# A softmax convolution with a cosine FFN: steady exponentials by arithmetic on ScalarE and POOL, a different order of PE's products in every other period, output sums in place

## The chip, the cores and the metric

The kernel runs on one core of one Trainium2 chip. The metric is the device time of one execution in microseconds (us); less is better. Engines are named as in the profile: PE (TensorE, with PEld for its weight loads), DVE (VectorE), ACT (ScalarE), POOL (GpSimd) and SP (SyncE, which issues the DMAs).

## The reference

Two stages. The first mixes, for every token and head, the last 7 tokens with softmax weights; the second is an FFN whose activation is h·cos(h).

```python
# x (8, 4096, 192), weight_gen (8, 4096, 8 heads, 7 taps)
w = weight_gen - np.max(weight_gen, axis=-1, keepdims=True)
w = np.exp(w)
w = w / (np.sum(w, axis=-1, keepdims=True) + 1e-09)
x_pad = np.concatenate([np.zeros((B, pad, D)), x], axis=1)     # pad = 6
x_unf = x_pad[:, idx, :].reshape(B, S, K, H, group)            # the 7 last rows
out = np.einsum('bshk,bskhg->bshg', w, x_unf)                  # (B*S, 192) = x of the FFN
...
h = x @ w_in            # 192 x 2048
g = h * np.cos(h)
return g @ w_out        # 2048 x 192
```

## The kernel before

**Tiling.** The 32768 tokens are laid out as 128 partitions by 256 rows. A block is 4 rows (`R`), 512 tokens; there are 64 blocks (`NB`). The 2048 hidden features are 16 chunks of 128, taken two at a time: 8 pairs (`NPAIR`). The main loop runs over `i`, one *period* for each block and pair, 512 periods and a tail; `b, pair = divmod(i, 8)`. Matmuls are split into a leading part and a remainder (`x_hi`, `x_lo`; `ghi`, `glo`; `wa_hi`, `wa_lo` and so on).

**A period.** PE makes the hidden products of pair `i` in two groups, `ffn_in_first` (L339) and `ffn_in_second` (L356), into one of three PSUM tiles `h`, and eight periods later (`LAG`) the output products of pair `j = i - 8` (`ffn_out`, L430) into the PSUM tile `acc`. Between them lies the cosine: ACT `turn` (L366, h in whole turns as an integer), DVE fraction (L370), ACT sine (L374), DVE product (L377), ACT `ghi` (L384), DVE `glo` (L388). The last one frees the `h` tile, and PE's first product three periods later takes it again.

**Groups of four.** `k` is the place of `j` within four output periods, and equals `i` modulo 4. After k=1 ACT copies the transposed row out of `acc` into `xrow` and writes zeros over it (L446, L447 in `evacuate`); after k=3 it copies `acc` into `part` (L452) and POOL adds its two halves into `fin` (L461), which SP stores three periods later. The row of the next block but one is transposed by PE inside the output products (L318), then split by ACT (`x_hi`, L296) and POOL (`x_b`, L298, and `x_lo`, L301).

**PE's order in a period** is set in `products` (L597). With k=0 the period begins with the first hidden product, then all output products; with k=1, 2, 3 it begins with most of the output products, then the first hidden product, then the rest of the output products. The second hidden product is last in both.

**The first stage.** POOL forms the convolution of a block in 7 products (L255) and 6 sums (L270), two operations a period, under `bg`. The weights of 16 rows (four blocks) come from one `softmax` (L185): a DMA of `taps`, the maximum on DVE (L198), the subtraction on POOL (L200), `Exp` on ACT (L203), the sums on POOL (`add_taps`), a reciprocal on DVE (L214), and the final product on POOL (L220). It is a generator, moved on one step by the loop at the steps listed in `SOFTMAX`, once every 32 periods; `early=False` marks the 15 softmaxes of the loop. Around the `Exp` of step 6 the loop has special cases (`exps`, `early_sums`, held-back `splits`).

Every engine works through its instructions in the order in which the program issues them; a chain of dependencies at the end of the program fixes that order. SP stands between PE's product groups: `traded` (L281) lets PE's next group into a tile only after SP has seen the one before finished.

Of the kernel before, what the change touches and what calls it, by code (L numbers as in the profile page):

```python
# [11 lines left out]
F32 = mybir.dt.float32  # L12
F32R = mybir.dt.float32r
I32 = mybir.dt.int32
U16 = mybir.dt.uint16
BF16 = mybir.dt.bfloat16
AF = mybir.ActivationFunctionType
ALU = mybir.AluOpType
AX = mybir.AxisListType

P = 128
TWO_PI = 2.0 * math.pi
# [15 lines left out]


F64_SCALE = 2.0 ** -112  # L40


@with_exitstack
def tile_softmax_conv_then_cos_ffn(
# [8 lines left out]
    nc = tc.nc  # L53

    B, S, D = x.shape
    H, K = weight_gen.shape[2], weight_gen.shape[3]
# [5 lines left out]
    R = 4  # L62
    NB = RPP // R
# [3 lines left out]
    RW = 16  # L67
    SB = RW // R
    NPAIR = NFC // 2
# [10 lines left out]
    work = ctx.enter_context(tc.tile_pool(name="work", bufs=2))  # L80
# [6 lines left out]
    o_v = out.rearrange("(n q r) d -> q n (r d)", n=B, r=RPP)  # L87

    ident = const.tile([P, P], F32, name="ident")
    early = const.tile([P, 1], F32, name="early")  # L90
# [83 lines left out]
    taps, ready = {}, set()  # L174

    def add_taps(t, out):
        three_ = work.tile([P, RW * H, 3], F32, name="three", bufs=1)
        three = three_[:, 0:t.shape[1]]
        nc.gpsimd.tensor_tensor(out=three, in0=t[:, :, 0:3], in1=t[:, :, 3:6], op=ALU.add)
        old = three[:, :, 0]  # L180
        for more in (three[:, :, 1], three[:, :, 2], t[:, :, 6]):
            nc.gpsimd.tensor_tensor(out=out, in0=old, in1=more, op=ALU.add)
            old = out

    def softmax(r0, r1, eng, early=True, to=None):  # L185
        n = (r1 - r0) * H
        if r0 == 0:
            t = const.tile([P, n, K], F32, name="taps0")
        else:
            tile_ = work.tile([P, RW * H, K], F32, name="taps")  # L190
            t = tile_[:, 0:n, :]
        nc.sync.dma_start(out=t.rearrange("p a k -> p (a k)"), in_=g_v[:, :, r0 * H * K:r1 * H * K])
        for b in range(r0 // R, r1 // R):
            taps[b] = t.rearrange("p (r h) k -> p r h k", h=H)[:, b * R - r0:(b + 1) * R - r0]
        yield
        top_ = work.tile([P, RW * H], F32, name="top", bufs=1)
        top = top_[:, 0:n]
        nc.vector.tensor_reduce(out=top, in_=t, axis=AX.X, op=ALU.max)  # L198
        yield
        eng.tensor_tensor(  # L200
            out=t, in0=t, in1=top.unsqueeze(2).broadcast_to([P, n, K]), op=ALU.subtract)
        yield
        nc.scalar.activation(out=t, in_=t, func=AF.Exp)  # L203
        yield
        den_ = work.tile([P, RW * H], F32, name="den")
        den = den_[:, 0:n]
        if early:
            nc.vector.tensor_reduce(out=den, in_=t, axis=AX.X, op=ALU.add)
        else:
            add_taps(t, den)  # L210
        (nc.vector if early else nc.gpsimd).tensor_scalar(
            out=den, in0=den, scalar1=1e-9, scalar2=TWO_PI, op0=ALU.add, op1=ALU.mult)
        yield
        nc.vector.reciprocal(out=den, in_=den)  # L214
        yield
        m = 0 if to is None else to.shape[1]
        if m:
            eng.tensor_tensor(
                out=to, in0=t[:, 0:m], in1=den[:, 0:m].unsqueeze(2).broadcast_to([P, m, K]), op=ALU.mult)
        eng.tensor_tensor(  # L220
            out=t[:, m:], in0=t[:, m:], in1=den[:, m:].unsqueeze(2).broadcast_to([P, n - m, K]),
            op=ALU.mult)
        ready.update(range(r0 // R, r1 // R))
# [167 lines left out]
    accs, stores, splits = {}, {}, []  # L391
# [48 lines left out]
    def evacuate(j):  # L440
        b, tp, k = place(j)
        acc = accs[b, tp]
        row = row_of(j)
        if k == 1 and row:
            t = work.tile([P, 2, P], F32, name="xrow", bufs=2)
            nc.scalar.copy(out=t, in_=acc[:, :, 2 * D:])  # L446
            nc.scalar.copy(out=acc[:, :, 2 * D:], in_=zero.unsqueeze(2).broadcast_to([P, 2, P]))  # L447
        if k == 3:
            accs.pop((b, tp))
            part = work.tile([P, 2, CT], F32, name="part", bufs=2)  # L450
            width = CT if row else 2 * D
            nc.scalar.copy(out=part[:, :, 0:width], in_=acc[:, :, 0:width])  # L452
            t = part[:, :, 2 * D:]
        if k in (1, 3) and row:
            bt, r = row
            splits.append(split(bt, t, slice(r * P, (r + 1) * P), nc.gpsimd))
        if k < 3:
            return
        last = b == NB - 1
        fin = work.tile([P, 2, D], F32, name="fin")  # L460
        (nc.vector if last else nc.gpsimd).tensor_tensor(  # L461
            out=fin, in0=part[:, :, 0:D], in1=part[:, :, D:2 * D], op=ALU.add)

        def store():
            r0 = b * R + 2 * tp
            nc.sync.dma_start(out=o_v[:, :, r0 * D:(r0 + 2) * D],
                              in_=fin.rearrange("p r d -> p (r d)"))

        if last:
            store()  # L470
        else:
            stores[j + LATE] = store
        if tp == 1:
            for pair in range(NPAIR):
                g_parts.pop(b * NPAIR + pair)
# [59 lines left out]
    def go_on(steps, n):  # L535
        for _ in range(n):
# [4 lines left out]
                      t=own_taps.rearrange("p (r h) k -> p r h k", h=H))  # L541
# [28 lines left out]
    N = NB * NPAIR  # L570

    sm = sm2
    EXP = 6
    SOFTMAX = (0, 2, 3, EXP, 7, 12, 13)
    for i in range(N + LAG + 1):
        b, pair = divmod(i, NPAIR)
        j = i - LAG
        step = i % (SB * NPAIR) - (SB - 1) * NPAIR
        if step < 0 and i >= SB * NPAIR:
            step += SB * NPAIR  # L580
        if step == 0 and b + 4 < NB:
            r0 = (b + 4) * R
            sm = softmax(r0, min(r0 + RW, RPP), nc.gpsimd, early=False)
        busy = b + 4 < NB if step < NPAIR else b + 3 < NB
        exps = busy and step == EXP
        converts_now = converts.get(i, ())
        if converts_now:
            make_room()

        whole = None  # L590
        if pair == TR and b + 1 <= WHOLE:
            until_mixed(b + 1)
            whole = transpose_all(b + 1)
        if 0 <= j and (i - ROWS_AT) % (2 * R) == 0 and row_of(j):
            until_mixed(row_of(j)[0])

        def products():  # L597
            if b < NB and pair == 0:
                assert b in transposed
            if whole is not None and j >= 0:  # L600

                ffn_out(j)
                ffn_in_first(i, whole)
            elif i < N and j >= 0 and j % R != 0:

                ffn_out(j, rest=False)
                ffn_in_first(i)
                ffn_out(j, rest=True)
            else:
                if i < N:  # L610
                    ffn_in_first(i, whole)
                if j >= 0:
                    ffn_out(j)
            if i < N:
                ffn_in_second(i)
            if j in stores:
                stores.pop(j)()
            if j >= 0:
                evacuate(j)


        early_sums = busy and step == EXP + 1
        if 0 <= i - 1 < N:
            act_turns(i - 1)
        if early_sums:
            products()
        if 0 <= i - 2 < N:
            act_hi(i - 2)
        all_of(*converts.pop(i - 1, ()))
        if exps:  # L630
            next(sm)
        now, later = [], []
        if not (busy and EXP + 1 <= step <= EXP + 3):
            now = list(splits)
            splits.clear()
        if whole is not None:
            t = work.tile([P, 2, CT], F32, name="part", bufs=2)
            nc.scalar.copy(out=t, in_=whole)
            later.append(split(b + 1, t, slice(0, CT), nc.vector))
        if 0 <= i - 1 < N:  # L640
            dve_fraction(i - 1)
            act_cos(i - 1)
        for c in now:
            next(c)
        splits.extend(later)
        if 0 <= i - 2 < N:
            dve_lo(i - 2)
        if 0 <= i - 1 < N:
            dve_g(i - 1)
        for _ in range(4):  # L650
            for c in converts_now:
                next(c)
        all_of(*now)
        if i == N + LAG:
            break
        if not early_sums:
            products()
        load_weights(i)
        if step in SOFTMAX and step != EXP or NPAIR - 2 <= i < NPAIR + 1:
            next(sm, None)  # L660
        for _ in range(3 if i < 12 or i < 64 and i % 4 == 0 else 2):
            next(bg, None)
# [41 lines left out]
```

## Time and profile before

| | |
|---|---|
| median of 3 runs | 2293.05 us (2292.56 to 2294.24) |
| profiled execution, its own time | 2294.02 us |
| its span | 2292.2 us |
| mean granted TensorE clock | 0.984 |
| instructions | 61619 |

A span is the time from the first to the last instruction of the profiled execution; the execution's own time is a little longer. Rows of the timeline give start, duration, engine, line and operation, `out<-in`, and in brackets the idle time before with what ended it. Rows of groups give count, total busy time, mean in ns, and the idle time before.

### The profile page before, as it was taken

Reading aid. Unit: us, or ns where it says so; the run is one execution under the profiler, and the core shown is the slowest. Engines: PE = TensorE matmul, PEld = TensorE weight load, DVE = VectorE, ACT = ScalarE, POOL = GpSimd, SP = SyncE. Lnnn points to the kernel's source line nnn. Section 1 sums busy time; section 2 is a strip of 40 time slices with the busy share of each in tenths; the row PEclk is TensorE's granted clock in tenths of the full one; section 3 lists DMA queues with packets and bytes.
Section 4 is the critical chain, followed back from the end, with each engine's and each line's share of the span. In section 5 each row is a group of like instructions: output and inputs, shape, how many; then the busy total and the mean of one; then the engine's idle time right before and its main releaser. Section 6 shows DMA issues by size and latency. Waiting matters only on the chain.

```text
span 2292.2 us, 61619 instructions
## 1 busy us (share of the span) xinstructions
PE 2187.0 (95%) x26472; PEld 1679.2 (73%) x26472; DVE 1903.1 (83%) x1644; ACT 1860.6 (81%) x2254; POOL 1860.8 (81%) x1583
## 2 busy tenths in 40 slices
PE   2699999999999999999999999999999999999998
PEld 1477777777777777777777777777777777777777
DVE  7788888878888888888888888888888888888886
ACT  4688888888888888887888888888888888888885
POOL 8788878888888878879888888878879888788730
PEclk8799999999999999999999999999999999999999
DMA  6221221211211221221211211111121211212100
GB/s 154 56 54 29 50 54 29 58 46 29 58 47 37 50 49 35 50 55 29 58 40 36 54 40 47 47 43 44 47 49 38 54 33 46 54 33 48 29 15 18
DMA packets 34847, 105.61 MB, mean 46 GB/s; under 512 B 3742, under 2 KB 23702, under 8 KB 34574
## 3 DMA queue, kind: packets, MB, share of 16 engines
q1 hardware_dynamic: 34574, 101.68, 18.5%
q8 instruction: 207, 3.39, 0.6%
q14 instruction: 66, 0.54, 0.1%
HBM read 76.50 MB, written 25.17 MB: 44 GB/s over the span
## 4 chain that ended last, share of the span: by engine, by line
PE 83%; ACT 7%; DVE 7%; issue 2%; POOL 1%; DMA 0%; SPq 0%; ACTq 0%; DVEq 0%
PE acc L430 42%; PE h L356 25%; PE h L339 13%; DVE turn L370 3%; ACT turn L366 3%; DVE glo L388 2%; ACT part L452 1%; PE acc L318 1%; ACT turn L374 1%; ACT ghi L384 1%; DVE den L214 1%; ACT acc L447 0%; ACT xrow L446 0%; POOL xa L270 0%; PE h L430 0%
## 5 line engine op out<-in xcount | busy, mean ns | idle before, releaser
L370 DVE TENSOR_TENSOR turn<-h,turn 128x1024 f32<-128x1024 f32 x512 | 625.9, 1222 | 302.0 <-ACT turn L366 301.9
L430 PE MATMUL acc<-wo,ghi 64*128 64x384 f32 x8096 | 821.6, 341 | 3.6 <-ACT acc L447 2.5
L430 PEld LDWEIGHTS acc<-wo,ghi 64*128 64x128 f32 x8096 | 726.2, 186 | 89.0 <-ACT acc L447 56.4
L270 POOL TENSOR_TENSOR xa<-xa,pr 128x768 f32<-128x768 f32 (+1 forms) x384 | 698.2, 1818 | 0.7
L374 ACT ACTIVATE turn<-turn 128x1024 f32<-128x1024 f32 x512 | 542.0, 1059 | 186.6 <-DVE turn L370 184.8
L366 ACT ACTIVATE turn<-h 128x1024 int32<-128x1024 f32 x512 | 525.9, 1027 | 194.3 <-PE h L356 176.9
L377 DVE SCALAR_TENSOR_TENSOR h<-h,turn 128x1024 f32<-128x1024 f32 x512 | 631.0, 1232 | 54.4 <-ACT turn L374 54.4
L388 DVE TENSOR_TENSOR glo<-h,ghi 128x1024 bf16<-128x1024 f32 x512 | 622.0, 1215 | 10.1 <-ACT ghi L384 10.1
L255 POOL TENSOR_TENSOR pr<-xt,taps 128x768 f32<-128x768 f32 (+1 forms) x384 | 588.3, 1532 | 8.3
L384 ACT CAST ghi<-h 128x1024 fp32r<-128x1024 f32 x512 | 516.7, 1009 | 9.7 <-DVE h L377 9.7
L430 PE MATMUL acc<-wo_b,glo 64*128 64x192 bf16 x8096 | 489.0, 245 | 0.1
L430 PEld LDWEIGHTS <-glo 64*128 64x128 bf16 (+1 forms) x8128 | 315.9, 95 | 118.6 <-issue 100.5
L298 POOL TENSOR_SCALAR x_b<-x_hi 128x256 bf16<-128x256 f32 (+1 forms) x247 | 102.9, 417 | 261.8 <-ACT x_hi L296 261.8
L339 PE MATMUL h<-x_hi,wa_hi 64*128 64x512 f32 x1024 | 302.9, 587 | 0.0
L356 PE MATMUL h<-x_hi,wa_hi 64*128 64x512 f32 x1024 | 302.7, 586 | 0.0
L339 PE MATMUL h<-x_lo,wa_b 64*128 64x512 bf16 x1024 | 198.3, 382 | 71.0 <-DVE glo L388 66.1
L356 PE MATMUL h<-x_hi,wb_hi 64*128 64x512 f32 x1024 | 205.5, 396 | 0.0
L461 POOL TENSOR_TENSOR fin<-part 128x384 f32<-128x384 f32 x126 | 128.1, 1016 | 86.2 <-ACT part L452 86.2
L356 PE MATMUL h<-x_lo,wa_b 64*128 64x512 bf16 x1024 | 196.8, 379 | 0.8
L339 PE MATMUL h<-x_b,wa_lo 64*128 64x512 bf16 x1024 | 197.2, 380 | 0.0
L356 PE MATMUL h<-x_b,wa_lo 64*128 64x512 bf16 x1024 | 197.0, 380 | 0.0
L356 PE MATMUL h<-x_lo,wb_b 64*128 64x512 bf16 x1024 | 196.8, 379 | 0.0
(78 smaller groups left out, 1869.2 us busy)
## 6 DMA issues: line engine op xcount, KB each, us to landing
xt<-in_x_dram SPq DMA_DIRECT2D x62, 960.0 KB, 6.9
out_dram<-fin SPq DMA_DIRECT2D x128, 192.0 KB, 2.5
taps<-in_weight_gen_dram SPq DMA_DIRECT2D x15, 448.0 KB, 4.7
raw<-in_moe_w_out_dram SPq DMA_DIRECT2D x8, 384.0 KB, 4.4
raw<-in_moe_w_in_dram SPq DMA_DIRECT2D x10, 256.0 KB, 9.7
xt<-in_x_dram SPq DMA_DIRECT2D x1, 768.0 KB, 9.9
xt<-in_x_dram SPq DMA_DIRECT2D x1, 540.0 KB, 5.4
raw<-in_moe_w_in_dram SPq DMA_DIRECT2D x4, 128.0 KB, 5.0
```

Of the source, the lines that this page charges most:

```text
L255: eng.tensor_tensor(out=dst.rearrange("p r (h g) -> p r h g", h=H), in0=xt[:, k + ra:k + rb, :].rearrange("p r (h g) -> p r h g", h=H), in ...
L270: eng.tensor_tensor(out=acc if k < K else xa, in0=acc, in1=old[:, ra:rb], op=ALU.add)
L339: nc.tensor.matmul(h[:, q, :], lhsT=w[rs, chunk(pair, q)], rhs=v[rs, q, :], start=(m == 0), stop=False, skip_group_check=True)
L356: nc.tensor.matmul(h[:, 1 - q, :], lhsT=w[rs, cs], rhs=v[rs, q ^ middle, :], start=False, stop=(m == len(prods) - 1), skip_group_check=True)
L366: nc.scalar.activation(out=t.bitcast(I32), in_=hs[i], func=AF.Identity, bias=0.25, scale=1.0)
L370: nc.vector.tensor_tensor(out=t, in0=hs[i], in1=t.bitcast(I32), op=ALU.subtract)
L374: nc.scalar.activation(out=t, in_=t, func=AF.Sin, bias=SIN_BIAS, scale=SIN_SCALE)
L377: nc.vector.scalar_tensor_tensor(out=hs[i], in0=hs[i], scalar=TWO_PI, in1=turns.pop(i), op0=ALU.mult, op1=ALU.mult)
L384: nc.scalar.copy(out=hi, in_=hs[i])
L388: nc.vector.tensor_tensor(out=lo, in0=hs.pop(i), in1=hi.bitcast(F32), op=ALU.subtract)
L430: nc.tensor.matmul(to, lhsT=g[rs, n, t * P:(t + 1) * P], rhs=w[rs, fc, :], start=(lo == 0 and c == 0 and (k == 0 or whole and k == 1)), st ...
L461: (nc.vector if last else nc.gpsimd).tensor_tensor(out=fin, in0=part[:, :, 0:D], in1=part[:, :, D:2 * D], op=ALU.add)
```

## The change

1. **The exponential.** In the 15 softmaxes of the loop, `Exp` on ACT is replaced by `powers`: exp(t) = 2^n · e^r, with n the whole number nearest t/ln 2 (ACT, written as an integer), r = t - n ln 2 (POOL), a polynomial for e^(r/2) as a product of two squares with added constants (squares on ACT, the rest on POOL), squared once more (ACT), and 2^n made by writing n into the exponent bits (ACT `Relu` with a scale and a bias). The polynomial's leading factor cancels in the quotient, so that the small constant in the denominator is divided by `EXP_UNIT`. Ahead of it POOL limits t to at least -100. All of it goes in halves of 448 elements a partition, a few operations at a time, each step in a period of its own.
2. **When.** A softmax now starts at period 9 modulo 32 and moves one step every period, up to period 30. The special cases around the `Exp` are gone.
3. **PE's order.** The period begins with the first hidden product for k=0 and k=2, no longer for k=0 alone.
4. **Buffers.** The output sum is written over the first half of `part`, and is stored in two DMAs; `xrow` has one buffer instead of two; the scratch tile `three` becomes part of `side`, and `whole` is new.

```diff
+EXP_A = ((0.2721300161859934, 6.259058152201904), (1.7341319627121385, 0.787141348722592))
+EXP_UNIT = 0.04161451162765518 ** 2
+EXP_LEAST = -100.0
+LN_2 = math.log(2.0)
+ONE_BITS = float(127 * 2 ** 23)
...
     def add_taps(t, out):
-        three_ = work.tile([P, RW * H, 3], F32, name="three", bufs=1)
-        three = three_[:, 0:t.shape[1]]
+        three_ = work.tile([P, RW * H, K], F32, name="side", bufs=1)
+        three = three_[:, 0:t.shape[1], 0:3]
...
+    def powers(t):
+
+        (a1, b1), (a2, b2) = EXP_A
+        n = t.shape[1]
+        whole_ = work.tile([P, RW * H, K], I32, name="whole", bufs=1)
+        side_ = work.tile([P, RW * H, K], F32, name="side", bufs=1)
+        cut = (slice(0, n // 2), slice(n // 2, n))
+        t, whole, side = ([v[:, c] for c in cut] for v in (t, whole_, side_))
+
+        def near(k):
+            nc.scalar.activation(out=whole[k], in_=t[k], func=AF.Identity, scale=1.0 / LN_2)
+
+        def rest(k):
+            nc.gpsimd.tensor_scalar(
+                out=side[k], in0=whole[k], scalar1=-LN_2, scalar2=1.0, op0=ALU.mult, op1=ALU.mult)
+            nc.gpsimd.tensor_tensor(out=t[k], in0=side[k], in1=t[k], op=ALU.add)
+
+        def square(k, to, a):
+            nc.scalar.activation(out=to[k], in_=t[k], func=AF.Square, bias=a, scale=0.5)
+
+        def quartic(k):
+            nc.gpsimd.tensor_scalar(
+                out=side[k], in0=side[k], scalar1=b1, scalar2=1.0, op0=ALU.add, op1=ALU.mult)
+            nc.gpsimd.tensor_scalar(
+                out=t[k], in0=t[k], scalar1=b2, scalar2=1.0, op0=ALU.add, op1=ALU.mult)
+            nc.gpsimd.tensor_tensor(out=t[k], in0=t[k], in1=side[k], op=ALU.mult)
+
+        def power(k):
+            nc.scalar.activation(
+                out=whole[k], in_=whole[k], func=AF.Relu, bias=ONE_BITS, scale=2.0 ** 23)
+
+        def again(k):
+            nc.scalar.activation(out=t[k], in_=t[k], func=AF.Square)
+
+        def product(k):
+            nc.gpsimd.tensor_tensor(out=t[k], in0=t[k], in1=whole[k].bitcast(F32), op=ALU.mult)
+
+        near(0)
+        yield
+        near(1)
+        rest(0)
+        yield
+        rest(1)
+        yield
+        yield
+        square(0, side, a1)
+        yield
+        square(0, t, a2)
+        yield
+        square(1, side, a1)
+        quartic(0)
+        yield
+        square(1, t, a2)
+        yield
+        power(0)
+        quartic(1)
+        yield
+        power(1)
+        yield
+        again(0)
+        yield
+        again(1)
+        product(0)
+        yield
+        product(1)
+        yield
...
-        yield
-        nc.scalar.activation(out=t, in_=t, func=AF.Exp)
-        yield
+        if early:
+            yield
+            nc.scalar.activation(out=t, in_=t, func=AF.Exp)
+            yield
+        else:
+            eng.tensor_scalar(
+                out=t, in0=t, scalar1=0.0, scalar2=EXP_LEAST, op0=ALU.min, op1=ALU.max)
+            yield
+            yield
+            yield
+            yield from powers(t)
...
-            t = work.tile([P, 2, P], F32, name="xrow", bufs=2)
+            t = work.tile([P, 2, P], F32, name="xrow", bufs=1)
...
-        fin = work.tile([P, 2, D], F32, name="fin")
+        fin = part[:, :, 0:D]
         (nc.vector if last else nc.gpsimd).tensor_tensor(
-            out=fin, in0=part[:, :, 0:D], in1=part[:, :, D:2 * D], op=ALU.add)
+            out=fin, in0=fin, in1=part[:, :, D:2 * D], op=ALU.add)
...
-            nc.sync.dma_start(out=o_v[:, :, r0 * D:(r0 + 2) * D],
-                              in_=fin.rearrange("p r d -> p (r d)"))
+            for n in range(2):
+                nc.sync.dma_start(out=o_v[:, :, (r0 + n) * D:(r0 + n + 1) * D], in_=fin[:, n, :])
...
-    EXP = 6
-    SOFTMAX = (0, 2, 3, EXP, 7, 12, 13)
+    FIRST = NPAIR + 1
...
-        if step == 0 and b + 4 < NB:
-            r0 = (b + 4) * R
+        if i % (SB * NPAIR) == FIRST and b + 6 < NB:
+            r0 = (b + 6) * R
             sm = softmax(r0, min(r0 + RW, RPP), nc.gpsimd, early=False)
...
-            elif i < N and j >= 0 and j % R != 0:
+            elif i < N and j >= 0 and j % 2 != 0:
...
-        if step in SOFTMAX and step != EXP or NPAIR - 2 <= i < NPAIR + 1:
+        if i >= NPAIR - 2:
             next(sm, None)
```

How the instructions move, at the places of which the prediction speaks. On ACT before, around one exponential of the loop (L366 is `turn`, L374 the sine, L384 `ghi`, L446 and L447 the copy and the zeroing after k=1):

```order
L446 COPY xrow<-acc 128x256
L447 COPY acc<-zero 128x2x128
L366 ACTIVATE turn<-h 128x1024
L384 CAST ghi<-h 128x1024
L203 ACT_TABLE_LOAD
L203 ACTIVATE taps<-taps 128x896
L374 ACT_TABLE_LOAD
L374 ACTIVATE turn<-turn 128x1024
```

On ACT now, the second and third of four squares of one softmax (L451 is `turn`, L459 the sine, L469 `ghi`, L537 the copy of `acc`, L381 `x_hi`, L210 a square):

```order
L537 COPY part<-acc 128x1024
L210 ACTIVATE taps<-taps 128x448
L451 ACTIVATE turn<-h 128x1024
L469 CAST ghi<-h 128x1024
L459 ACTIVATE turn<-turn 128x1024
L381 CAST x_hi<-part 128x2x128
L210 ACTIVATE side<-taps 128x448
```

The two table loads and the 896-element `Exp` between `ghi` and the sine are gone; half-size operations stand at the end of a period, behind the copies and splits and ahead of the next `turn`.

On PE before, the boundary into a k=2 period (L356 ends the period before; L430 is the output product, L318 the row's transposes):

```order
L356 MATMUL h<-x_b,wb_lo 128x512
L356 MATMUL h<-x_hi,wa_hi 128x512 x2
L356 MATMUL h<-x_hi,wb_hi 128x512 x2
L430 MATMUL acc<-wo,ghi 128x384 x16
L318 MATMUL acc<-ident,xa 128x64 x2
L430 LDWEIGHTS glo
```

On PE now, at the same place (L441 ends the period before, L424 is the first hidden product, L515 the output product, L403 the transposes):

```order
L441 MATMUL h<-x_hi,wb_hi 128x512 x2
L424 LDWEIGHTS wa_b
L424 MATMUL h<-x_lo,wa_b 128x512
L424 LDWEIGHTS wa_b
L424 MATMUL h<-x_lo,wa_b 128x512
L424 LDWEIGHTS wa_lo
L424 MATMUL h<-x_b,wa_lo 128x512
L424 LDWEIGHTS wa_lo
L424 MATMUL h<-x_b,wa_lo 128x512
L424 MATMUL h<-x_hi,wa_hi 128x512 x2
L515 MATMUL acc<-wo,ghi 128x384 x16
L403 MATMUL acc<-ident,xa 128x64 x2
```

The six matmuls of the first hidden product have moved ahead of the sixteen that write into `acc`.

On POOL now, the first operations of `powers` in the queue (L546 is the output sum, L205 and L207 the remainder r, L340 and L355 a product and a sum of the convolution):

```order
L546 TENSOR_TENSOR part<-part 128x2x192
L205 TENSOR_SCALAR side<-whole 128x448
L207 TENSOR_TENSOR taps<-side,taps 128x448
L340 TENSOR_TENSOR pr<-xt,taps 128x768
L355 TENSOR_TENSOR xa<-xa,pr 128x768
```

They stand between the output sum and the convolution's next two operations, which follow the output sum directly where no softmax is under way.

More of the change, by code (lines that the diff above doesn't have):

```diff
@@ L211, in softmax @@
         (nc.vector if early else nc.gpsimd).tensor_scalar(
-            out=den, in0=den, scalar1=1e-9, scalar2=TWO_PI, op0=ALU.add, op1=ALU.mult)
+            out=den, in0=den, scalar1=1e-9 / (1.0 if early else EXP_UNIT), scalar2=TWO_PI,
+            op0=ALU.add, op1=ALU.mult)
         yield
+        if not early:
+            yield
         nc.vector.reciprocal(out=den, in_=den)
@@ L577, in tile_softmax_conv_then_cos_ffn @@
         j = i - LAG
-        step = i % (SB * NPAIR) - (SB - 1) * NPAIR
-        if step < 0 and i >= SB * NPAIR:
-            step += SB * NPAIR
-        if step == 0 and b + 4 < NB:
-            r0 = (b + 4) * R
+        if i % (SB * NPAIR) == FIRST and b + 6 < NB:
+            r0 = (b + 6) * R
             sm = softmax(r0, min(r0 + RW, RPP), nc.gpsimd, early=False)
-        busy = b + 4 < NB if step < NPAIR else b + 3 < NB
-        exps = busy and step == EXP
         converts_now = converts.get(i, ())
@@ L619, in products @@
                 evacuate(j)
-        early_sums = busy and step == EXP + 1
         if 0 <= i - 1 < N:
             act_turns(i - 1)
-        if early_sums:
-            products()
         if 0 <= i - 2 < N:
@@ L629, in tile_softmax_conv_then_cos_ffn @@
         all_of(*converts.pop(i - 1, ()))
[L630 to L635, printed above, removed]
+        now, later = list(splits), []
+        splits.clear()
         if whole is not None:
@@ L655, in tile_softmax_conv_then_cos_ffn @@
             break
-        if not early_sums:
-            products()
+        products()
         load_weights(i)
-        if step in SOFTMAX and step != EXP or NPAIR - 2 <= i < NPAIR + 1:
+        if i >= NPAIR - 2:
             next(sm, None)
```

## The prediction

> **What bounds the kernel now.** First the page: its head, the busy times and the chain that ended last.
> ```profile
> span 2292.2 us, 61619 instructions
> PE 2187.0 (95%) x26472; PEld 1679.2 (73%) x26472; DVE 1903.1 (83%) x1644; ACT 1860.6 (81%) x2254; POOL 1860.8 (81%) x1583
> PE 83%; ACT 7%; DVE 7%; issue 2%; POOL 1%; DMA 0%; SPq 0%; ACTq 0%; DVEq 0%
> ```
> The last line is the chain's: PE carries 83% of the span, and another engine matters only where PE waits for it. So I look for the time in which PE is not in its plain rhythm. The next view has busy times by stretch (columns: length, then PE, PEld, DVE, ACT, POOL, the granted clock, DMA share, GB/s).
> ```profile
> 899.10:1175.56 276.46, 271.00 (x3328) 209.18 (x3328) 232.22 (x197) 230.36 (x279) 233.94 (x199) 0.99 0.19 45
> 1088.77:1105.59 16.82, 16.82 (x210) 12.94 (x210) 14.32 (x13) 13.98 (x17) 12.90 (x12) 1.00 0.31 71
> 1156.04:1175.56 19.52, 16.97 (x209) 13.19 (x208) 14.22 (x13) 17.12 (x20) 12.73 (x14) 1.00 0.27 62
> 1017.03:1038.12 21.09, 18.54 (x208) 14.74 (x208) 14.22 (x13) 17.11 (x20) 14.30 (x15) 0.92 0.24 57
> ```
> A period has 52 matmuls (6 of L339, 12 of L356, 32 of L430, 2 of L318), so the first stretch, 3328 matmuls, is 64 periods and holds two softmaxes. A quiet stretch of four periods takes 16.82 us; the same four periods with an exponential in them take 19.52 us one time and 21.09 us the next. At the quiet rate 64 periods are 16 x 16.82 = 269.1 us; the stretch has 276.46. The two softmaxes cost 7.3 us, 3.67 each. Why, the timeline and the groups show.
> ```profile
> 1019.02 1.28 ACT L203 ACT_TABLE_LOAD   x1
> 1020.31 0.95 ACT L203 ACTIVATE taps<-taps 128x896 f32<-128x896 f32 x1
> 1021.28 1.28 ACT L374 ACT_TABLE_LOAD   x1
> 1028.07 0.39 PE L339 MATMUL h<-x_lo,wa_b 64*128 64x512 bf16 x2 [2.50 <-DVE glo L388]
> L203 ACT ACT_TABLE_LOAD x15 | 19.2, 1283 | 0.3
> ```
> Two table loads and the Exp hold ACT for 3.5 us between two of its steady steps; two periods on PE waits 2.50 us for the buffer that DVE frees late. In 1017:1038 the granted clock is also down, 0.92 for the stretch, and PE's busy time is 18.54 against 16.97: another 1.6 us. Fifteen such events: 15 x 3.67 = **55.0 us**.
>
> [...]
>
> The quiet rhythm has a hole of its own.
> ```profile
> 1101.28 1.58 PE L430 MATMUL acc<-wo,ghi 64*128 64x384 f32 x16
> 1103.69 1.22 DVE L388 TENSOR_TENSOR glo<-h,ghi 128x1024 bf16<-128x1024 f32 x1
> 1105.15 0.38 ACT L447 COPY acc<-zero 128x256 f32<-128x256 f32 x1
> 1105.58 1.36 PEld L430 LDWEIGHTS acc<-wo,ghi 64*128 64x128 f32 x16 [0.43 <-ACT acc L447]
> 1109.82 1.57 PE L430 MATMUL acc<-wo,ghi 64*128 64x384 f32 x16
> 1113.96 0.39 PE L339 MATMUL h<-x_lo,wa_b 64*128 64x512 bf16 x2
> 1116.05 0.22 PE L318 MATMUL acc<-ident,xa 64*128 64x64 f32 x2
> 1118.10 1.58 PE L430 MATMUL acc<-wo,ghi 64*128 64x384 f32 x16
> L447 ACT COPY acc<-zero 128x256 f32<-128x256 f32 x122 | 45.8, 375 | 3.9
> ```
> These are the starts of k=1, 2, 3, 0 and 1: 4.30, 4.24, 4.14, 4.14 us apart. The k=2 period begins with the output product, whose weight load waits for ACT's zeroing of the accumulator (L447). That costs 0.16 before its start and 0.10 after it (loads no longer ahead): 0.26 us, 122 times, 31.7 us. Without it four periods take 16.56 us.
>
> **The change, part by part.** *Exp removed.* The order of the changed program has two table loads in all, both before the loop, so all 15 pairs go: -55.0 us. What is late next is below.
>
> *First product first at k=2.* PE then has 0.7 us of input product in front (1113.96 to 1114.64 in k=0 today), while L447 ends 0.11 us after the unstalled start (1105.53 against 1105.42) and the load is wanted about 0.45 after it. The wait is covered: **-31.7 us**. The price is an earlier need of h: glo ended at 1104.91, 0.5 us before that start. Today's slack at k=2 was 2.3 us.
>
> Floor: 2292.2 - 55.0 - 31.7 = 2205.5 us.
>
> *ACT's ten half-batch operations.* They stand behind ACT's other work of a period, ahead of the next `turn`.
> ```profile
> 1101.48 1.03 ACT L366 ACTIVATE turn<-h 128x1024 int32<-128x1024 f32 x1 [0.43 <-PE h L356]
> 1105.63 1.03 ACT L366 ACTIVATE turn<-h 128x1024 int32<-128x1024 f32 x1
> 1110.03 1.03 ACT L366 ACTIVATE turn<-h 128x1024 int32<-128x1024 f32 x1 [0.72 <-PE h L356]
> 1114.20 1.03 ACT L366 ACTIVATE turn<-h 128x1024 int32<-128x1024 f32 x1
> 1116.52 1.06 ACT L374 ACTIVATE turn<-turn 128x1024 f32<-128x1024 f32 x1 [0.39 <-DVE turn L370]
> 1117.48 0.39 ACT L296 CAST x_hi<-part 128x256 fp32r<-128x256 f32 x1
> L203 ACT ACTIVATE taps<-taps x18: 389/952/952, 4.1 to 2126.2; 128x896 f32<-128x896 f32 x15, 128x224 f32<-128x224 f32 x2, 128x448 f32<-128x448 f32 x1
> ```
> From 389 ns at 224 and 952 at 896 elements, 448 take 577 ns; queued operations overlap by 0.1 (1116.52 + 1.06 against 1117.48), so one adds 0.48. ACT needs 4.15 us (k=1: 1101.48 to 1105.63) and 4.17 (k=3: 1110.03 to 1114.20) in periods that copy an accumulator, and 3.58 in the others (1114.20 to 1117.48, and 0.39 less 0.1). Against 4.14 us an added operation makes them +0.49, +0.51 and -0.08. The operations fall on periods 14, 15 and 18 to 25 of a softmax (periods counted modulo 32, k modulo 4). From 18: lateness 0, 0.5 (k=3), 0.4, 0.9 (k=1), 0.85, then more. A late `turn` makes glo late by as much, and PE feels it only where the next period starts with the input product (next k=0 or 2), beyond 0.43 us of slack (`turn` follows PE by 0.21, glo ends 3.43 later, 4.14 - 3.64 = 0.50, less a hand-over). That gives 0.4 us before period 24 and 0.45 before 26; L447, late too, adds about 0.2 at k=2. **1.1 us a softmax.** Bounds: 0, and 10 x 0.48 = 4.8 if all stood on the path.
>
> *POOL.* Busy 233.94 / 2 = 117.0 us per softmax of 32 periods; at the new rate 32 periods are 132.5 us.
> ```profile
> L255 POOL TENSOR_TENSOR pr<-xt,taps 128x768 f32<-128x768 f32 x378 | 585.2, 1548 | 8.3
> L270 POOL TENSOR_TENSOR xa<-xa,pr 128x768 f32<-128x768 f32 x378 | 694.7, 1838 | 0.6
> L270 POOL TENSOR_TENSOR xa<-xa,pr 128x192 f32<-128x192 f32 x6 | 3.5, 586 | 0.1
> L200 POOL TENSOR_TENSOR taps<-taps,top 128x448 f32<-128x448 f32 x1 | 1.0, 971 | 2.7 <-DVE top L198 2.7
> L144 POOL TENSOR_TENSOR wb_lo<-t,wb_hi 128x512 bf16<-128x512 f32 x2 | 2.5, 1270 | 0.0
> L298 POOL TENSOR_SCALAR x_b<-x_hi 128x256 bf16<-128x256 f32 x244 | 99.8, 409 | 258.7 <-ACT x_hi L296 258.7
> L298 POOL TENSOR_SCALAR x_b<-x_hi 128x1024 bf16<-128x1024 f32 x3 | 3.1, 1047 | 3.1 <-ACT x_hi L296 3.1
> L301 POOL TENSOR_TENSOR x_lo<-part,x_hi 128x256 bf16<-128x256 f32 x122 | 90.4, 741 | 0.0
> L461 POOL TENSOR_TENSOR fin<-part 128x384 f32<-128x384 f32 x126 | 128.1, 1016 | 86.2 <-ACT part L452 86.2
> 1029.32 0.93 POOL L179 TENSOR_TENSOR three<-taps 128x384 f32<-128x384 f32 x1
> 1032.38 1.54 POOL L255 TENSOR_TENSOR pr<-xt,taps 128x768 f32<-128x768 f32 x1
> ```
> Six two-tensor operations of 448: between 586 at 192 and 1838 at 768 lies 1.14 us (bounds 0.97, with one operand repeated, and 1.27, at 512). Six scalar ones: between 409 and 1047, 0.57 (bounds 0.41, and 0.97 if int32 words cost like a second tensor); one at 896 (period 11), 0.94. Added: 6.8 + 3.4 + 0.9 = 11.2 us; POOL 128.2 of 132.5. It fits, but unevenly. In period 15 it waits for ACT's accumulator copy, 4.5 us after the start. From there to the last sum of period 27 it has 11 products and 11 sums (37.2), 6 splits (409 + 741: 6.9), 4 output sums (4.1), 12 new operations (10.3) and the denominator (1029.32 to 1032.38, 3.1): 61.6 us, so it ends 4.5 + 61.6 - 12 x 4.14 = 16.4 us after period 27 starts. PE wants that result at its row transposes of period 30 (k=2), 12.4 + 2.1 (1113.96 to 1116.05) = 14.5. Late by 1.9, less the 0.9 by which ACT has already held PE back before period 27: 1.0. Consecutive operations overlap a little at their ends, which this sum leaves out and which could take all of it; I take **0.2**. Bounds: 0, and at the upper prices 6 x 0.40 + 6 x 0.13 = 3.2 more, 3.4. DVE's reciprocal of period 29 waits for the same queue.
>
> *Once.* At the start POOL runs without a gap, and the subtraction and clamp of the first softmax (about twice the 971 ns at 448, and 0.9) now stand before sums that PE wants: 0 to 2.8, taken 1.4. *The rest.* The in-place output sum is the same operation as L461; the single `xrow` buffer is read by POOL two to three periods before ACT writes it again; the store's second DMA issue lies on SP, beside PE. Each is 0 while POOL stays under three periods (12.4 us) behind those readers, and otherwise shares POOL's price.
>
> **Sum.** Fourteen full softmaxes x 1.3 = 18.2; the fifteenth has a quarter of the columns and no weight. 2205.5 + 18.2 + 1.4 = 2225.1 us of span. The profiled execution took 2294.02 for its span of 2292.2 (+1.8) and stands 0.97 above the median 2293.05: 2225.1 + 1.8 - 1.0 = **2226 us**.
>
> **Rivals.** *ACT and POOL keep up.* If PE's 0.43 us of slack is really larger and POOL overlaps better, only the floor and a little are left: 2205.5 + 1.4 + 0.8 = 2208. For it: POOL idles 258.7 us on x_hi today; against it: ACT has nothing to spare in k=1 and k=3. *POOL is late in earnest.* At the upper prices it costs 3.4 us in one wait at period 30: 14 x 3.4 = 48 more than ACT's 15.4, and a clock loss of 1.6 in every second, 11: 2205.5 + 15.4 + 48 + 11 + 2.2 = 2282; halfway, 2250. *The reorder gives nothing*, because glo at k=2 is always later than the L447 wait was: 2226 + 32 = 2258. The 0.5 us seen speaks against it. *Slower:* POOL becomes the bound, PE and DVE's reciprocal following its queue for all 32 periods. A softmax takes 276.46 / 2 = 138.2 us today; POOL exceeds that when the addition is over 21.2 us, 1.9 times my price. At twice, 139.4: 2293 + 14 x 1.2 = 2310. No row of POOL is near such a price.
>
> **How the numbers follow.** Forecast (2214 to 2240) 0.52, keeping up 0.18, POOL late 0.2, no reorder gain 0.05, slower 0.04, about nothing 0.01. Range 2207 to 2264: it leaves out the upper half of POOL late, and slower. Faster by over 0.2% 0.95, same 0.01, slower 0.04; 0.2% (4.6 us) is about what a measurement of this kernel can tell from no change.
>
> **What would show it.** Right: no ACT_TABLE_LOAD in the loop; no 2.5 us wait of L339's successor; clock 1.00 at every softmax; quiet four periods 16.56; small waits of PE on DVE glo in periods 24 and 26. Wrong: four quiet periods at 16.8 (reorder), PE waiting on POOL at the row transposes or DVE's reciprocal on POOL's den (POOL late), POOL's 448 operations above 1.27 or 0.97, or ACT waiting for POOL in the new operations.

## The result, and the profile after

| | before | after |
|---|---|---|
| median of the runs | 2293.64 us | 2235.31 us |
| range | 2292.56 to 2294.43 | 2234.16 to 2235.84 |
| span of the profiled execution | 2292.2 us | 2232.4 us |
| its own time | 2294.02 us | 2234.16 us |

The ratio is 0.9745, 95% interval 0.9728 to 0.9762. Forecast were 2226 us and a range of 2207 to 2264.

The page of the changed kernel, its head, busy times and chain:

```profile
span 2232.4 us, 62070 instructions
PE 2154.0 (96%) x26472; PEld 1669.4 (75%) x26472; DVE 1905.9 (85%) x1644; ACT 1871.8 (84%) x2359; POOL 2014.8 (90%) x1778
PE 56%; POOL 38%; issue 2%; ACT 2%; DVE 2%; DMA 0%; SPq 0%; POOLq 0%; ACTq 0%; DVEq 0%
```

POOL's busy time has grown by 154 us, and the chain that ended last now runs through POOL for 38% of the span, where it had 1%. Whether POOL really set the end is a matter of how far PE waited for it. The busy times of a quiet stretch of four periods and of 32 periods, one softmax (columns: length, PE, PEld, DVE, ACT, POOL, granted clock, DMA share, GB/s):

```profile
1206.43:1222.98 16.55, 16.55 (x211) 13.26 (x209) 14.33 (x13) 14.96 (x20) 15.66 (x15) 1.00 0.30 72
1142.00:1276.10 134.10, 133.29 (x1666) 104.57 (x1664) 116.27 (x99) 116.03 (x147) 127.65 (x113) 1.00 0.19 46
```

Quiet periods run at the forecast rate, 16.55 us for four, and the clock stays at 1.00 through a softmax. At that rate 32 periods are 132.4 us; the stretch has 134.10. So 1.7 us a softmax are left, where the prediction had 1.3. Where they are, the starts of the second hidden product of consecutive periods tell: the excess of each interval over 4.1375 us, the mean of 11 softmaxes (the 4th to the 14th), listed where it is over 0.03 us. An entry at 29 is lost between that product of period 29 and that of period 30.

```
kernel               excess by period (us)                                        a softmax
before               1 to 29, every fourth: 0.26 to 0.46;   31: 3.36                5.76
after                11: 0.16   23: 0.41   25: 0.17   29: 0.95                      1.70
```

The rows behind these entries, in one softmax of the changed kernel (timeline: start, duration, engine, line, operation, in brackets the idle time before and what ended it):

```profile
1186.20 1.08 DVE L272 TENSOR_REDUCE top<-taps 128x128 f32<-128x896 f32 x1
1189.40 1.00 ACT L537 COPY part<-acc 128x1024 f32<-128x1024 f32 x1
1190.45 1.35 PEld L515 LDWEIGHTS acc<-wo,ghi 64*128 64x128 f32 x16 [0.31 <-ACT part L537]
1206.86 1.02 POOL L546 TENSOR_TENSOR part<-part 128x384 f32<-128x384 f32 x1 [0.34 <-ACT part L537]
1239.48 0.99 ACT L537 COPY part<-acc 128x1024 f32<-128x1024 f32 x1
1240.52 1.36 PEld L515 LDWEIGHTS acc<-wo,ghi 64*128 64x128 f32 x16 [0.35 <-ACT part L537]
1247.07 1.22 DVE L473 TENSOR_TENSOR glo<-h,ghi 128x1024 bf16<-128x1024 f32 x1
1248.34 0.10 PEld L424 LDWEIGHTS <-wa_b 64*128 64x128 bf16 x2 [0.38 <-DVE glo L473]
1265.71 0.30 POOL L293 TENSOR_SCALAR den<-den 128x128 f32<-128x128 f32 x1
1266.04 0.95 DVE L299 RECIPROCAL den<-den 128x128 f32<-128x128 f32 x1 [0.38 <-POOL den L293]
1266.09 1.83 POOL L355 TENSOR_TENSOR xa<-xa,pr 128x768 f32<-128x768 f32 x1
1267.97 0.28 PE L403 MATMUL acc<-ident,xa 64*128 64x64 f32 x2 [0.77 <-POOL xa L355]
```

In periods 12 and 24 (both k=0) PE's output product waits for ACT's copy of the accumulator, which ends at 1190.40 and 1240.47, 0.05 us before the product's first weights are loaded. At 12 the copy is late because DVE's maximum (1186.20), issued in period 10, delays the fraction, and so the sine that stands ahead of the copy on ACT; at 24 it is late because of the operations that were added on ACT. Before 26 (k=2) glo is late: it ends at 1248.29 and the first hidden product follows at 1248.34. In period 30 PE's transposes wait for the convolution's last sum, which stands on POOL behind the softmax's denominator. The reciprocal waits in the same queue.

### The profile page after: what moved, and what is told of

It reads as the page before. It is cut to its first block, busy times and chain, and to the rows that moved or that the text cites. A ratio compares the mean times of both kernels' runs of the same rounds, so it can differ in the third digit from the quotient of the medians.

```text
span 2232.4 us, 62070 instructions
## 1 busy us (share of the span) xinstructions
PE 2154.0 (96%) x26472; PEld 1669.4 (75%) x26472; DVE 1905.9 (85%) x1644; ACT 1871.8 (84%) x2359; POOL 2014.8 (90%) x1778
## 4 chain that ended last, share of the span: by engine, by line
PE 56%; POOL 38%; issue 2%; ACT 2%; DVE 2%; DMA 0%; SPq 0%; POOLq 0%; ACTq 0%; DVEq 0%
PE acc L515 28%; PE h L441 18%; POOL xa L355 13%; POOL pr L340 10%; PE h L424 9%; POOL x_lo L386 3%; POOL part L546 2%; POOL taps L217 1%; POOL taps L227 1%; POOL taps L207 1%; POOL x_b L383 1%; POOL den L189 1%; POOL xa L340 1%; PE acc L403 1%; POOL taps L215 1%
## 5 line engine op out<-in xcount | busy, mean ns | idle before, releaser
L515 PE MATMUL acc<-wo,ghi 64*128 64x384 f32 x8096 | 805.2, 336 | 0.3 <-ACT ghi L469 0.2
L515 PEld LDWEIGHTS acc<-wo,ghi 64*128 64x128 f32 x8096 | 724.5, 184 | 52.8 <-ACT part L537 10.8
L459 ACT ACTIVATE turn<-turn 128x1024 f32<-128x1024 f32 x512 | 541.7, 1058 | 212.1 <-DVE turn L455 212.1
L355 POOL TENSOR_TENSOR xa<-xa,pr 128x768 f32<-128x768 f32 (+1 forms) x384 | 698.5, 1819 | 1.7
L451 ACT ACTIVATE turn<-h 128x1024 int32<-128x1024 f32 x512 | 523.9, 1023 | 104.8 <-PE h L441 88.1
L340 POOL TENSOR_TENSOR pr<-xt,taps 128x768 f32<-128x768 f32 (+1 forms) x384 | 588.0, 1532 | 4.9
L469 ACT CAST ghi<-h 128x1024 fp32r<-128x1024 f32 x512 | 516.8, 1009 | 2.9 <-DVE h L462 1.3
L515 PE MATMUL acc<-wo_b,glo 64*128 64x192 bf16 x8096 | 462.2, 243 | 0.1
L515 PEld LDWEIGHTS <-glo 64*128 64x128 bf16 (+1 forms) x8128 | 318.1, 94 | 85.3 <-issue 67.4
L441 PE MATMUL h<-x_hi,wa_hi 64*128 64x512 f32 x1024 | 301.7, 585 | 0.0
L424 PE MATMUL h<-x_hi,wa_hi 64*128 64x512 f32 x1024 | 301.6, 584 | 0.0
L424 PE MATMUL h<-x_lo,wa_b 64*128 64x512 bf16 x1024 | 199.4, 385 | 37.7 <-DVE glo L473 32.9
L441 PE MATMUL h<-x_hi,wb_hi 64*128 64x512 f32 x1024 | 204.2, 395 | 0.0
L441 PE MATMUL h<-x_lo,wa_b 64*128 64x512 bf16 x1024 | 196.3, 379 | 0.8
L424 PE MATMUL h<-x_b,wa_lo 64*128 64x512 bf16 x1024 | 197.1, 380 | 0.0
L441 PE MATMUL h<-x_b,wa_lo 64*128 64x512 bf16 x1024 | 196.5, 380 | 0.0
L441 PE MATMUL h<-x_lo,wb_b 64*128 64x512 bf16 x1024 | 196.4, 379 | 0.0
L441 PE MATMUL h<-x_b,wb_lo 64*128 64x512 bf16 x1024 | 196.3, 379 | 0.0
```

The source lines that it names most:

```text
L340: eng.tensor_tensor(out=dst.rearrange("p r (h g) -> p r h g", h=H), in0=xt[:, k + ra:k + rb, :].rearrange("p r (h g) -> p r h g", h=H), in ...
L355: eng.tensor_tensor(out=acc if k < K else xa, in0=acc, in1=old[:, ra:rb], op=ALU.add)
L424: nc.tensor.matmul(h[:, q, :], lhsT=w[rs, chunk(pair, q)], rhs=v[rs, q, :], start=(m == 0), stop=False, skip_group_check=True)
L441: nc.tensor.matmul(h[:, 1 - q, :], lhsT=w[rs, cs], rhs=v[rs, q ^ middle, :], start=False, stop=(m == len(prods) - 1), skip_group_check=True)
L451: nc.scalar.activation(out=t.bitcast(I32), in_=hs[i], func=AF.Identity, bias=0.25, scale=1.0)
L459: nc.scalar.activation(out=t, in_=t, func=AF.Sin, bias=SIN_BIAS, scale=SIN_SCALE)
```

## Experiments

All times are medians, each ratio with its interval against runs of the kernel before on the same chip. On these chips the kernel before took 2293.4 to 2295.5 us, so one or two us between the medians of two experiments say little; the lists of excess by period, made as above, tell them apart better.

**PE's order put back (order_back).** One line of the changed kernel:

```diff
-            elif i < N and j >= 0 and j % 2 != 0:
+            elif i < N and j >= 0 and j % R != 0:
```

> The changed kernel with PE's old order at k=2 (only k=0 begins with the hidden product). Theory, the zeroing of the accumulator is what PE waits for at k=2: four quiet periods go back from 16.55 to 16.82 us, 122 x 0.26 = 31.7 us more, less the waits of 0.17 us before period 26 that the early need of h causes (14 x 0.17 = 2.4): about 2264 us. Rival, the gain of the changed kernel is all the exponential's: no change, 2235 us.

2258.87 us, 0.9845 [0.983, 0.986]. The wait is back in all 122 places, as the waits of this kernel show (total us, times, longest):

```profile
PEld acc L515 <- ACT acc L532: 64.1, 122, 0.8
```

Excess: 0.27 in most of the fourth periods, 0.67, 0.66 and 0.59 at 21, 25 and 29; 3.27 a softmax against 1.70. The order is worth some 24 us here (23.6 between the medians, 24.9 between the spans), less than 31.7: eight waits of 0.27 are 2.16, and the waits of ACT, DVE and POOL beside them have gone down from 1.70 to 1.11, so part of them lies under the order's wait.

**PE's order alone (order_only).** The same line, changed in the kernel before.

> The kernel before with the new order at k=2 alone, Exp and its table loads kept. Theory: quiet four periods 16.55 us, each softmax still some 3.7 us, 2293.6 - 31.7 = 2262 us. Rival, the earlier need of h at k=2 meets the late glo after the Exp and gives much of it back: 2270 us or more.

2270.29 us, 0.9892 [0.9878, 0.9907]. The quiet wait is gone, but the Exp now costs more, 3.95 us at 31 and 0.17 at 27, 4.10 a softmax: PE wants h earlier and waits 2.77 us for it instead of 2.50, and the clock goes down after 11 of the 15 waits (0.87 over the 13 us around each), where it did after 7 in the kernel before. That is the rival's side: 25 us in place of 31.7.

**The softmax two periods later (shift2).**

```diff
-    FIRST = NPAIR + 1
+    FIRST = NPAIR + 3
```

> The changed kernel with each softmax of the loop started two periods later (period 11 instead of 9), so that POOL's denominator falls behind period 27 and the result that PE wants at period 30 no longer waits for it. Theory, PE's wait of 0.95 us at period 30 is POOL's backlog at that place: it goes, 14 x 0.95 = 13 us and some of the first softmax's 3.4 us, 2219 to 2222 us. Rival, POOL is simply full over its 32 periods: the wait moves to another place, 2235 us.

2238.6 us, 0.9758 [0.9742, 0.9774]: a miss; the rival, that the wait only moves, holds. The wait at period 30 is gone, as the theory had it; in its place stands another at the start of period 0.

```profile
1275.40 0.39 PE L424 MATMUL h<-x_lo,wa_b 64*128 64x512 bf16 x2 [1.44 <-POOL x_lo L386]
```

Excess: 0.17 at 25, 0.43 at 27, 1.60 at 31, 2.22 a softmax against 1.70. POOL's backlog now passes the sum in time, but not the row's split two periods on, which PE wants as well. ACT's two waits moved by the two periods of the edit, but not with their sizes: the larger again stands at the start of a k=0 period (28), where PE needs the copy of the accumulator, the smaller at a k=2 one. DVE's 0.16 is gone; its maximum now falls ahead of a k=2 period.

**The limit of t left out (no_clamp).** The `tensor_scalar` with `EXP_LEAST` is taken out.

> The changed kernel without the limit of t on POOL (0.94 us a softmax, in period 11; left out). Theory, POOL catches up and waits for ACT between periods 11 and 15, so that only what it does from 15 to 27 counts: the wait at period 30 stays 0.95 us and only the start gains, 0 to 2 us, 2233 to 2235 us. Rival, POOL's whole load counts: 14 x 0.94 = 13 us less, 2222 us.

2233.73 us, 0.9736 [0.9721, 0.975]. Excess 0.95 at 29, 1.72 a softmax, as with it: 0.94 us less of POOL in period 11 buys nothing there, so it isn't POOL's load over 32 periods that counts. Only the first softmax gains: its excess at 30 goes from 1.91 to 0.91.

**POOL's four additions left out (no_adds).** Two `tensor_scalar` of `quartic` are taken out, for both halves.

> The changed kernel without POOL's four scalar additions of the polynomial (4 x 0.565 = 2.26 us a softmax, in periods 20 and 22; left out). Theory, POOL's queue between period 15 and 27 sets PE's wait at period 30: 0.95 us is gone, and so is DVE's wait for the denominator; 14 x 0.95 = 13 us and 2 us of the first softmax, 2218 to 2222 us, with ACT's waits before periods 24 and 26 as they were. Rival, the wait at period 30 has another cause (ACT's or DVE's lateness): no change, 2235 us.

2218.56 us, 0.9668 [0.9654, 0.9683]. Excess 0.16 at 11, 0.41 at 23, 0.16 at 25, nothing at 29: 0.74. 2.26 us less between periods 15 and 27 take the whole wait of 0.95 away. With no_clamp this places the cause: POOL's queue in that stretch.

**ACT's last two squares left out (no_again).**

> The changed kernel without ACT's last two squares (periods 24 and 25; left out). Theory: PE's 0.41 us before period 24 comes from the operations of 18 to 23 and stays, the 0.17 us before period 26 goes; but PE's wait at period 30 is for POOL, which does not get earlier, so that it grows by the same 0.17: the sum of a softmax stays 1.7 us, 2234 to 2236 us. Rival, the waits add up: 14 x 0.17 = 2.4 us less, 2233 us; the per-period excess tells the two apart.

2235.64 us, 0.9742 [0.9726, 0.9758]. Excess 0.16 at 11, 0.42 at 23, none at 25, 1.16 at 29: 1.74. The waits of this kernel at the transposes, and the changed kernel's:

```profile
PEld acc L403 <- POOL xa L355: 16.1, 13, 1.3
PE acc L403 <- POOL xa L355: 12.0, 13, 1.0
```

```profile
PEld acc L403 <- POOL xa L355: 13.6, 13, 1.1
PE acc L403 <- POOL xa L355: 9.5, 13, 0.8
```

What ACT gives back before 26, POOL takes at 30. As forecast by the theory, the two waits don't add up: PE is only as early at period 30 as POOL lets it be.

**Two periods earlier, after the first (earlier2).**

```diff
     FIRST = NPAIR + 1
+    EARLY = 2
...
-        if i % (SB * NPAIR) == FIRST and b + 6 < NB:
-            r0 = (b + 6) * R
+        if (i == FIRST or i > FIRST and i % (SB * NPAIR) == FIRST - EARLY) and i // 32 * 4 + 7 < NB:
+            r0 = (i // 32 * 4 + 7) * R
```

> The changed kernel with the softmaxes after the first started two periods earlier (7 instead of 9). Theory, a queue summed up from the measured durations: POOL is 1.3 us ahead of PE's want at period 30 and within 0.5 us of the row's split that is wanted two periods after it, so 0.95 becomes 0 to 0.4; ACT's 0.58 moves to before periods 22 and 24, DVE's 0.16 to before 10: 1.0 us a softmax, 2224 to 2229 us. Rival, POOL is full and the wait only moves, as it did for the later start: 2235 us or more.

2219.21 us, 0.9672 [0.9658, 0.9687]: more than expected. Excess 0.16 at 21 and 0.43 at 23 and no more, 0.61 a softmax. POOL's wait is gone and no other came; so is DVE's of 0.16, which had been expected to move along: as in shift2, the maximum now falls ahead of a k=2 period. ACT's larger wait again stands before a k=0 period (24).

**The steps spread out (spread).** The changed kernel with the softmaxes after the first from period 6; the maximum a period after the load, the subtraction two periods after it, and more blank periods between the steps of `powers` (`EARLY` is 3, the loop's condition as in earlier2):

```diff
         near(0)
         yield
+        yield
         near(1)
         rest(0)
         yield
+        yield
         rest(1)
         yield
-        yield
         square(0, side, a1)
         yield
+        yield
         square(0, t, a2)
...
         again(0)
         yield
+        product(0)
+        yield
         again(1)
-        product(0)
         yield
         product(1)
...
+        if not early:
+            yield
```

> The changed kernel with the same operations spread over periods 6 to 34 (the first softmax from 9): ACT's ten never more than two in three periods, POOL's in steps further apart, the maximum on DVE in an odd period. Theory, every one of the waits is a queue that is too dense for some periods: ACT's 0.58, DVE's 0.16 and POOL's 0.95 all go, 14 x 1.7 = 24 us and part of the first softmax's 3, 2209 to 2213 us. Rival, POOL's 128 of 132.5 us a softmax leaves no room: about 1 us a softmax stays, 2224 us or more.

2207.31 us, 0.9619 [0.9605, 0.9634], the fastest of all; no interval shows an excess. Its head, and 32 periods of it:

```profile
span 2205.5 us, 62070 instructions
1088.77:1221.15 132.38, 132.38 (x1668) 104.14 (x1668) 116.20 (x99) 116.43 (x146) 127.77 (x113) 1.00 0.19 47
```

POOL is as busy as before the spread, 127.77 us, now of 132.38, and PE never stops in them. The same operations on the same engines now cost PE nothing: what they cost before lay in their places. Of the 1.70 us a softmax, 1.09 went with the earlier start alone (earlier2); the other 0.61, ACT's, went with the spacing and one period more. The start gains too: the first softmax, which in the changed kernel held PE up by 1.9 and 1.5 us in two periods, has no such wait here, though it starts in the same period.

**The spread with PE's old order (spread_order_back).**

> The spread schedule with PE's old order at k=2. Theory: the wait for the accumulator's zeroing is worth its full 0.26 us where nothing else holds PE back: 122 x 0.26 = 31.7 us more than the spread kernel, 2207.3 + 31.7 = 2239 us, quiet four periods 16.82 in all of a softmax. In the changed kernel the same edit measured less (23.6 us), since there ACT's and POOL's waits lie under it. Rival, the order is worth the 23 to 26 us that both other pairs showed: 2231 to 2233 us.

2239.99 us, 0.9769 [0.9752, 0.9785]: 32.7 us more than the spread kernel. With nothing else in the way the order is worth what the timeline said.

Not tried: the output sum in place, the two-DMA store and the single `xrow` buffer by themselves, and the table loads apart from the Exp. From the end of the last period's second hidden product the span runs on for 23.3 us before and 23.2 after, and no wait of PE, ACT, DVE or POOL in the changed kernel names the store.

## Why the prediction was right, and where its size was off

| term (us of span) | predicted | measured |
|---|---|---|
| Exp and its table loads | -55.0 | -54.3 between the spans of before and spread_order_back (2292.2, 2237.9); no load in the loop, clock 1.00 |
| first product first at k=2 | -31.7 | -32.4 between the spans of spread and spread_order_back (2205.5, 2237.9) |
| floor | 2205.5 | 2205.5 (spread) |
| ACT, a softmax | 1.1 | 0.58 |
| POOL, a softmax | 0.2 | 0.95 |
| DVE's maximum, a softmax | not seen | 0.16 |
| once | 1.4 | 3.1, what is left of the span: start and first two softmaxes |
| span | 2225.1 | 2232.4 |

**Both gains** came out as worked out from the stretches of the profile before. The first difference also holds the buffers and the operations that were added, which in the spread kernel cost PE nothing in its 32 periods. That the spread kernel's span equals the floor to the tenth is partly luck, since its start differs a little; that nothing is left in its 32 periods is not.

**Prices.** Every operation's price held, from sizes and forms that the trace had:

```profile
L227 POOL TENSOR_TENSOR taps<-taps,whole 128x448 f32<-128x448 f32 x28 | 32.7, 1166 | 0.0
L207 POOL TENSOR_TENSOR taps<-side,taps 128x448 f32<-128x448 f32 x28 | 32.0, 1142 | 2.3
L205 POOL TENSOR_SCALAR side<-whole 128x448 f32<-128x448 int32 x28 | 15.8, 565 | 2.1
L281 POOL TENSOR_SCALAR taps<-taps 128x896 f32<-128x896 f32 x14 | 13.1, 935 | 1.2
L220 ACT ACTIVATE whole<-whole 128x448 int32<-128x448 int32 x28 | 16.2, 578 | 0.0
```

Forecast were 1.14, 0.57, 0.94 and 577 ns. With integers at the input POOL's scalar operation took 565 ns (L205), where the same size in f32 took 564 (L213, L215); that closes the upper bound.

**ACT.** The sum of lateness gave 0.4 before period 24, 0.45 before 26 and 0.2 for late accumulator work. Measured are 0.41 and 0.17. The places are right, and no_again shows that the second hangs on the operations of 24 and 25. The path at 24 was another than forecast: it is not glo that sets the time there but ACT's copy of the accumulator, so that the agreement of 0.4 with 0.41 is luck. The same copy is why DVE's maximum costs 0.16 at 12, a term that the sum did not have. At 26 the size was too large by half a microsecond; why is not shown, though each estimate of lateness carried the one before it.

**POOL is the step that was mis-sized.** The sum of its queue from period 15 to 27 gave a result 1.0 us late at period 30. I then took 0.2, on the ground that operations overlap at their ends. Measured is 0.95. That the sum of 1.0 comes so near is in part two errors that cancel: the queue took 61.06 us (1206.86 to 1267.92) where the sum had 61.6, so overlaps (0.05 us where the product from 1209.70 to 1211.25 meets the sum from 1211.20), less the gaps between the small operations (0.09 us from 1208.52 to 1208.61), are worth some 0.5 us and not the 0.8 that I allowed; and ACT had held PE back by 0.58 us, not 0.9. Fourteen times 0.75 is 10.5 us; ACT's and DVE's terms give 5.0 back (14 x 0.36). The net 1.70 against 1.30 is 5.6 of the 7.3 us by which the span was off.

**Once.** The other 1.7 us are this term, 3.1 for 1.4. It was put down to sums that PE wants; the wait came by another path, DVE's reciprocal, which the prediction had only named as waiting for the same queue. In the first softmax:

```profile
193.08 0.95 DVE L299 RECIPROCAL den<-den 128x128 f32<-128x128 f32 x1 [3.90 <-POOL den L293]
196.29 0.39 PE L424 MATMUL h<-x_lo,wa_b 64*128 64x512 bf16 x2 [1.73 <-DVE glo L473]
199.95 0.39 PE L424 MATMUL h<-x_lo,wa_b 64*128 64x512 bf16 x2 [1.15 <-DVE glo L473]
```

POOL came into it with a backlog (no_clamp takes 1.0 us off it), DVE stood idle for 3.90 us before the reciprocal, and glo behind it was late for PE. The excess was 1.91 and 1.49 at 30 and 31, 2.4 over the steady 0.95. The second softmax does the same with 2.69 us of DVE's idling: 0.70 and 1.50, 1.2 over. From the third on DVE waits less than 0.4 us there, which costs PE nothing. Some 0.6 us, most of it before the first softmax, where the runs differ anyway, go the other way.

The other 2 us of the median's distance of 9.3 us from the forecast are no work: the median stood 1.15 us above the profiled execution's time, where it had stood 1 below.

**The signs.** Those for "right" appeared: no table load in the loop, no wait of 2.5 us, clock 1.00, 16.55 us for four quiet periods, glo late at 26. So did one of those for "wrong", POOL late: PE waited for it at the row transposes, and DVE's reciprocal waited for its den. The time stayed within the forecast (2214 to 2240 us) since this wait was 0.95 us and not 3.4.

**The rivals.** "Keep up" lost mainly through POOL, 0.95 of the 1.70 us; without POOL's wait, in no_adds and earlier2, 0.74 and 0.61 of ACT's and DVE's remained, 2219 us. Spread shows that keeping up needed no less work, only other periods. "POOL late in earnest" named the right place with too high a price. "The reorder gives nothing" is refuted twice over, though order_only shows a grain of it: with the Exp in the loop the earlier need of h takes some 0.5 us a softmax back, about half of it by the clock, which goes down after 11 of its waits and after 7 of those before. "POOL the bound" is refuted by the spread kernel.

## What to carry to other kernels

An engine at 97% of the period can still be free of cost if its work is spread evenly (POOL in spread, 127.77 of 132.38 us, no excess), and one at 90% of the span can hold up the critical engine if its work is bunched (POOL in the changed kernel, 0.95 us a softmax): sum its queue, at measured lengths, between the last point where it waited and the next result that is wanted; here that sum was within 0.6 us of 61. Moving bunched work can move the wait to the next result in line, as in shift2, or remove it, as in earlier2, so check every result that is wanted behind it, not only the one that waits now. Two waits on the critical engine do not add up where the second is for an engine that was not held by the first: in no_again the one before 26 went, 0.17 us, and the one at 30 grew from 0.95 to 1.16.

## What the runs showed of the hardware

The same 2.50 us wait of PE cost clock in every second softmax of the kernel before, from the third on, and never in the others. Ten microseconds from the start of the wait, with loss and without:

```profile
472.65:482.65 10.00, 7.50 (x80) 6.92 (x82) 6.88 (x7) 6.59 (x8) 9.60 (x10) 0.83 0.40 95
611.65:621.65 10.00, 7.51 (x98) 6.50 (x100) 8.43 (x8) 7.76 (x9) 9.60 (x10) 1.00 0.40 93
```

In the first of these stretches the wait ends at 475.15; 0.83 us later the granted clock is 0.50, for 3.41 us:

```profile
472.57:475.98 3.41, 0.91 (x10) 0.72 (x10) 2.82 (x3) 3.04 (x4) 3.41 (x3) 1.00 0.97 236
475.98:479.39 3.41, 3.41 (x33) 3.34 (x32) 3.41 (x4) 2.07 (x2) 3.09 (x6) 0.50 0.22 45
479.39:482.80 3.41, 3.41 (x46) 2.94 (x44) 0.88 (x2) 1.71 (x2) 3.33 (x2) 1.00 0.02 5
```

In the kernel before, the 120 matmuls around a wait keep PE busy for 10.84 to 10.89 us with the loss and 9.27 to 9.29 without. Over both kernels the loop has 30 of these waits, 15 in each; the clock went down after 18 of them, 7 before and 11 in order_only, and not after the other 12. Their length does not tell them apart: waits of 2.50 us stand on both sides in the kernel before, waits of 2.77 us in order_only, and the last of each kernel, shorter at 2.09 and 2.20 us, cost clock too. What does tell them apart is not shown, and no experiment here moved such a wait by itself.
